# Expert tiles past the 24th moved into one of eight code arms, chosen at run time by the number of tiles in use

## The chip, the cores and the metric

The kernel runs on one core of a Trainium2 chip. A core has five engines with an instruction queue each: TensorE (PE, whose weight loads the profile lists apart as PEld), VectorE (DVE), ScalarE (ACT), GpSimd (POOL) and SyncE (SP), beside 16 DMA engines. Each queue is read in order by a sequencer of its engine, and work on different engines is ordered by semaphores. The metric is the device time of one execution in microseconds; the kernel before takes 641.05 us (median of three runs, 640.5 to 641.71).

## The reference, cut to what matters

Two stages, all in float32. A causal linear attention with a decay per head makes `x` of 4 x 768 tokens with 512 channels. A mixture of experts with 8 experts follows, in which a token either takes the expert with its largest logit or keeps the expert of the token before it:

```python
for s in range(S):
    fresh_e = int(np.argmax(logits[b, s]))
    if s == 0 or local_gate[b, s] < 0.5:
        e = fresh_e
    else:
        e = prev_e if prev_e >= 0 else fresh_e
    prev_e = e
    ...
    h = np.maximum(x[b, s] @ w1[e], 0.0)      # 512 -> 1024
    out[b, s] = p[e] * (h @ w2[e])            # 1024 -> 512
```

Which expert gets how many of the 3072 tokens is known only when the kernel runs. With the reference's inputs its routing gives the eight experts 410, 373, 371, 423, 434, 362, 354 and 345 tokens. In tiles of 128 tokens, of one expert each, that is 4, 3, 3, 4, 4, 3, 3 and 3: 27 tiles. Any routing needs between 24 (`NT`) and 31 (`G`) tiles.

## The kernel before, in words

Three stages follow each other.

**Attention** (lines 103 to 249): 24 steps of 128 tokens. SP loads q, k and v, PE does the matmuls, and each step writes 128 rows of `x` to the buffer `x_dram` in device memory and leaves 9 logits per token.

**Routing** (lines 252 to 385): one chain of small DVE and PE operations. It finds every token's expert, gives each expert whole tiles, and leaves three tables with a column per tile: `gidx` (which row of `x_dram` stands in each place of the tile), `sidx` (where the result goes; an unused place has an index past the end, which the store skips) and `gate`, and a row `owner` with each tile's expert. `ends` holds the running sum of the experts' tiles, so its last column is the number of tiles in use.

**Experts** (lines 388 to 447): a loop over all 31 tiles, unrolled when the program is built. For tile g:

- `gather(g)` (line 402, POOL): an indirect DMA brings 128 rows of `x_dram` into `xg`, one of three buffers.
- `turn` (line 409, PE; line 411, DVE): four transposes into `ptm`, copied to `xtm`.
- `hidden` (line 421, PE; line 423, ACT): 32 matmuls into `ph`, in two halves, each followed by a Relu into `ht`.
- `output` (line 429, PE; line 431, DVE; line 432, POOL): 8 matmuls into `py`, a multiplication with the gate into `y`, and an indirect DMA that stores `y`'s rows in the output.
- `weights(g)` (lines 394 to 398, SP): loads the tile's expert number into a register and issues two DMAs of 2 MB for `w1` and `w2`, into one of two buffers by the parity of g. The condition `other` skips them where that buffer holds this expert already.

The order on each engine comes from a scheduler that sees the whole unrolled loop; on PE it is `ph` of tile g, `ptm` of tile g+1, `py` of tile g. A float32 matmul of the program stands in the profile as two weight loads and two matmuls, a transpose as one of each; so PE's `ph` of one tile is 64 matmul records, `py` 16 and `ptm` 4. Tiles 27 to 30 are computed like the others: their gather reads row 0 for every place, and their store skips every row.

Of the kernel before, what the change touches and what calls it, by code (L numbers as in the profile page):

```python
# [9 lines left out]
I32 = mybir.dt.int32  # L10
U32 = mybir.dt.uint32
ACT = mybir.ActivationFunctionType
ALU = mybir.AluOpType
# [10 lines left out]
E, F = 8, 1024  # L24
DT, FT = DM // P, F // P
N = B * S
NT = N // P
# [4 lines left out]
G = (N + E * (P - 1)) // P  # L32
# [7 lines left out]
def kernel(  # L40
# [9 lines left out]
    nc = tc.nc  # L50
    const = ctx.enter_context(tc.tile_pool(name="const", bufs=1))
    wts = ctx.enter_context(tc.tile_pool(name="wts", bufs=1))
    route = ctx.enter_context(tc.tile_pool(name="route", bufs=1))
# [9 lines left out]
    def w1_src(e):  # L63
        return w1[bass.ds(e, 1)].rearrange("o (t p) f -> p (o t) f", p=P)

    def w2_src(e):
        return w2[bass.ds(e, 1)].rearrange("o (t p) d -> p (o t) d", p=P)
# [46 lines left out]
    with tc.tile_pool(name="build", bufs=1) as build:  # L114
# [10 lines left out]
        for u in range(2):  # L125
            rows = slice(DH * u, DH * u + DH)
# [126 lines left out]
    sidx = route.tile([P, G], U32, name="sidx")  # L253
    gate = route.tile([P, G], F32, name="gate")
    owner = route.tile([1, G], I32, name="owner")
    with tc.tile_pool(name="rt", bufs=1) as rt, tc.tile_pool(name="pr", bufs=1, space=PSUM) as pr:
        lg = lt[:, :, :E]
        mx = rt.tile([P, NT], F32, name="mx")
# [67 lines left out]
        more = rt.tile([P, E, NT], F32, name="more")  # L326
        nc.vector.tensor_tensor(more, incl[:, :, NT - 1:NT].broadcast_to([P, E, NT]),
                                whole.unsqueeze(1).broadcast_to([P, E, NT]), ALU.is_gt)
        tiles = rt.tile([P, E], F32, name="tiles")
        nc.vector.tensor_reduce(tiles, more, axis=AX.X, op=ALU.add)  # L330
        ends = rt.tile([P, E], F32, name="ends")
# [23 lines left out]
        own = rt.tile([1, G, E], F32, name="own")  # L355
# [3 lines left out]
        nc.vector.tensor_reduce(own1, own, axis=AX.X, op=ALU.add)  # L359
        nc.vector.tensor_scalar(own1, own1, float(E - 1), None, ALU.min)  # L360
        nc.vector.tensor_copy(owner, own1)


        val = rt.tile([P, NT, 2, G], F32, name="val")
# [28 lines left out]
    def weights(g):  # L393
        e = experts[g] = nc.values_load(owner[0:1, g:g + 1], engines=[SP], min_val=0, max_val=E - 1,
                                        skip_runtime_bounds_check_because="an index of 8 experts")
        other = e != experts[g - 2]
        nc.sync.dma_start(out=w1t[g % 2], in_=w1_src(e), cond=other, cond_hint=False)
        nc.sync.dma_start(out=w2t[g % 2], in_=w2_src(e), cond=other, cond_hint=False)

    def gather(g):  # L400
        xg = moe.tile([P, DM], F32, name="xg", bufs=3)
        nc.gpsimd.indirect_dma_start(out=xg, out_offset=None, in_=x_dram[:, :],  # L402
                                     in_offset=bass.IndirectOffsetOnAxis(ap=gidx[:, g:g + 1], axis=0))
        return xg

    def turn(xg):
        pt = pm.tile([P, DT, P], F32, name="ptm")
        for d in range(DT):
            nc.tensor.transpose(pt[:, d], xg[:, P * d:P * d + P], ident)  # L409
        xt = moe.tile([P, DT, P], F32, name="xtm")  # L410
        nc.vector.tensor_copy(xt, pt)  # L411
        return xt

    def hidden(g, xt):
        ht = moe.tile([P, FT, P], F32, name="ht")
        for half in range(2):
            ph = pm.tile([P, FT // 2, P], F32, name="ph")
            for i in range(FT // 2):
                f = FT // 2 * half + i
                for d in range(DT):  # L420
                    nc.tensor.matmul(ph[:, i], lhsT=w1t[g % 2][:, d, P * f:P * f + P], rhs=xt[:, d],  # L421
                                     start=(d == 0), stop=(d == DT - 1))
            nc.scalar.activation(ht[:, FT // 2 * half:FT // 2 * half + FT // 2], ph, ACT.Relu)  # L423
        return ht

    def output(g, ht):
        py = pm.tile([P, DM], F32, name="py")
        for f in range(FT):
            nc.tensor.matmul(py, lhsT=ht[:, f], rhs=w2t[g % 2][:, f], start=(f == 0), stop=(f == FT - 1))  # L429
        y = moe.tile([P, DM], F32, name="y")  # L430
        nc.vector.tensor_scalar(y, py, gate[:, g:g + 1], None, ALU.mult)  # L431
        nc.gpsimd.indirect_dma_start(out=out, out_offset=bass.IndirectOffsetOnAxis(ap=sidx[:, g:g + 1], axis=0),  # L432
                                     in_=y, in_offset=None, bounds_check=N - 1, oob_is_err=False)

    weights(0)
    weights(1)
    rows = {g: gather(g) for g in range(2)}
    xt = turn(rows.pop(0))
    for g in range(G):
        if g + 2 < G:  # L440
            rows[g + 2] = gather(g + 2)
        ht = hidden(g, xt)
        if g + 1 < G:
            xt = turn(rows.pop(g + 1))
        output(g, ht)
        if g + 2 < G:
            weights(g + 2)


# [32 lines left out]
```

## Time and profile before

| | |
|---|---|
| median of three runs | 641.05 us (640.5 to 641.71) |
| the profiled execution: its own time | 640.74 us |
| its span, first to last instruction | 639.0 us |
| mean granted TensorE clock | 0.965 |
| instructions | 9717 |
| PE busy | 590.9 us, 92% of the span |
| DVE, ACT, POOL busy | 126.3, 72.6 and 130.4 us |
| attention and routing, to the first `ph` | 0 to 182.7 us |
| 31 expert tiles on PE | 182.7 to 631.0 us |
| after PE's last matmul | 631.0 to 639.0 us |

Busy time of PE is the time in which matmuls are in flight; the granted clock is the share of full speed that the chip allowed. In a row of a timeline stand start and length in us, engine, line, operation, and behind it in brackets how long the engine was idle before and what ended that. An engine's name with a q (SPq, POOLq, PEldq) is its sequencer: waits, register loads and branches, which are not counted as busy.

### The profile page before, as it was taken

Reading aid. Unit: us, or ns where it says so; the run is one execution under the profiler, and the core shown is the slowest. Engines: PE = TensorE matmul, PEld = TensorE weight load, DVE = VectorE, ACT = ScalarE, POOL = GpSimd, SP = SyncE. Lnnn points to the kernel's source line nnn. Section 1 sums busy time; section 2 is a strip of 40 time slices with the busy share of each in tenths; the row PEclk is TensorE's granted clock in tenths of the full one; section 3 lists DMA queues with packets and bytes.
Section 4 is the critical chain, followed back from the end, with each engine's and each line's share of the span. In section 5 each row is a group of like instructions: output and inputs, shape, how many; then the busy total and the mean of one; then the engine's idle time right before and its main releaser. Section 6 shows DMA issues by size and latency. Waiting matters only on the chain. (4 is left out here: it accounts for less than half of the span.)

```text
span 639.0 us, 9717 instructions
## 1 busy us (share of the span) xinstructions
PE 590.9 (92%) x4104; PEld 449.3 (70%) x4104; DVE 126.3 (20%) x269; ACT 72.6 (11%) x136; POOL 130.4 (20%) x149
## 2 busy tenths in 40 slices
PE   4989889894669999999999999999999999999994
PEld 4777777773667777777777777777777777777772
DVE  6533434326700000100001000100001000010000
ACT  1222222230000000001000000000101000000100
POOL 4565565300031111111111111111111111111000
PEclk9999999995579999999999999999999999999998
DMA  8999986310020295494691296159379197010000
GB/s 315 361 344 388 379 300 223 117 67 16 2 82 21 86 329 211 167 313 161 236 336 53 67 338 226 34 172 330 130 255 334 50 337 252 34 34 12 0 1 1
DMA packets 37675, 113.63 MB, mean 178 GB/s; under 512 B 3390, under 2 KB 3390, under 8 KB 34560
## 3 DMA queue, kind: packets, MB, share of 16 engines
q1 hardware_dynamic: 29216, 92.30, 40.6%
q0 software_dynamic: 4960, 14.43, 6.5%
q10 hardware_dynamic: 3456, 6.29, 2.6%
q8 instruction: 32, 0.52, 0.3%
q14 instruction: 11, 0.09, 0.0%
HBM read 171.73 MB, written 14.42 MB: 291 GB/s over the span
## 5 line engine op out<-in xcount | busy, mean ns | idle before, releaser
L421 PEld LDWEIGHTS ph<-xtm,w 128*128 128x128 f32 x1984 | 227.5, 193 | 14.4 <-issue 14.4
L421 PE MATMUL ph<-xtm,w 128*128 128x128 f32 x1984 | 227.7, 276 | 0.0
L429 PE MATMUL py<-w,ht 128*128 128x512 f32 x496 | 218.0, 592 | 0.0
L429 PEld LDWEIGHTS py<-w,ht 128*128 128x128 f32 x496 | 91.8, 190 | 103.8 <-issue 103.8
L423 ACT ACTIVATE ht<-ph 128x512 f32<-128x512 f32 x62 | 37.0, 597 | 442.4 <-PE ph L421 442.4
L432 POOL DMA_INDIRECT out_dram<-y,sidx x31 | 31.4, 1014 | 242.2 <-DVE y L431 242.2
L402 POOL DMA_INDIRECT xg<-x_dram,gidx x31 | 30.3, 978 | 200.9 <-PE ptm L409 140.3
L431 DVE TENSOR_SCALAR y<-py,gate 128x512 f32<-128x512 f32 x31 | 23.3, 751 | 206.8 <-PE py L429 206.8
L411 DVE COPY xtm<-ptm 128x512 f32<-128x512 f32 x31 | 21.5, 693 | 204.6 <-PE ptm L409 204.6
L174 DVE TENSOR_TENSOR sm<-ps,mask 128x512 f32<-128x512 f32 x48 | 30.9, 686 | 34.6 <-PE ps L171 34.5
L171 PE MATMUL ps<-inp 64*128 64x128 f32 x384 | 29.7, 297 | 8.4 <-DMA inp<-in_qkv_dram 8.4
L156 POOL TENSOR_TENSOR qd<-inp,lamq 128x512 f32<-128x512 f32 x20 | 25.5, 1274 | 44.6 <-PE po L184 29.8
L171 PEld LDWEIGHTS ps<-inp 64*128 64x128 f32 x384 | 24.9, 199 | 13.0 <-DMA inp<-in_qkv_dram 8.7
L188 PE MATMUL po<-sm,inp 128*64 128x128 f32 x384 | 27.1, 285 | 0.0
L409 PE MATMUL ptm<-ident,xg 128*128 128x128 f32 x124 | 19.6, 283 | 6.0 <-DMA xg<-x_dram,gidx 6.0
L159 POOL TENSOR_TENSOR kd<-inp,rev 128x512 f32<-128x512 f32 x20 | 20.8, 1043 | 13.2 <-DVE rev L138 6.3
L188 PEld LDWEIGHTS po<-sm,inp 128*64 128x64 f32 x384 | 21.2, 140 | 3.0 <-issue 0.2
L184 PE MATMUL po<-qd,kv 128*128 128x128 f32 x160 | 23.2, 288 | 0.0
L197 PE MATMUL pk<-inp,kd 128*128 128x128 f32 x160 | 23.2, 288 | 0.0
L191 ACT COPY xt<-po 128x512 f32<-128x512 f32 x24 | 14.1, 586 | 75.3 <-PE po L188 75.3
L197 PEld LDWEIGHTS pk<-inp,kd 128*128 128x128 f32 x160 | 19.4, 191 | 3.6 <-issue 3.3
L184 PEld LDWEIGHTS po<-qd,kv 128*128 128x128 f32 x160 | 19.4, 191 | 2.5 <-issue 0.2
(107 smaller groups left out, 204.2 us busy)
## 6 DMA issues: line engine op xcount, KB each, us to landing
w<-in_w_dram SPq DMA_DIRECT2D x66, 2048.0 KB
inp<-in_qkv_dram SPq DMA_DIRECT2D x24, 1024.0 KB
x_dram<-xn ACTq DMA_DIRECT2D x24, 256.0 KB
xg<-x_dram,gidx POOLq DMA_INDIRECT x31, 3.9
out_dram<-y,sidx POOLq DMA_INDIRECT x31, 2.8
wgt<-in_wg_dram SPq DMA_DIRECT2D x1, 18.0 KB
lamb<-in_lam_dram SPq DMA_DIRECT2D x1, 4.0 KB
```

The lines of the kernel that those rows point to most:

```text
L156: nc.gpsimd.tensor_tensor(qd, x[:, 0].rearrange("p (a i) -> p a i", i=P), lamq, ALU.mult)
L171: nc.tensor.matmul(ps[u][:, a], lhsT=kt[rows, a], rhs=qt[rows, a], start=True, stop=True)
L174: nc.vector.tensor_tensor(sm[:, u], ps[u], mask[:, u], ALU.mult)
L184: nc.tensor.matmul(po[:, a], lhsT=kv[:, a].rearrange("p u d -> p (u d)"), rhs=qd[:, a], start=(a == 0), stop=False, skip_group_check=True)
L188: nc.tensor.matmul(po[DH * u:DH * u + DH, a], lhsT=vn[:, a, u], rhs=sm[:, u, a], start=(not c and a == 0), stop=(a == A - 1), skip_group_c ...
L197: nc.tensor.matmul(pk[:, a], lhsT=kd[:, cols], rhs=x[:, 3, cols], start=True, stop=True)
L402: nc.gpsimd.indirect_dma_start(out=xg, out_offset=None, in_=x_dram[:, :], in_offset=bass.IndirectOffsetOnAxis(ap=gidx[:, g:g + 1], axis=0))
L421: nc.tensor.matmul(ph[:, i], lhsT=w1t[g % 2][:, d, P * f:P * f + P], rhs=xt[:, d], start=(d == 0), stop=(d == DT - 1))
L423: nc.scalar.activation(ht[:, FT // 2 * half:FT // 2 * half + FT // 2], ph, ACT.Relu)
L429: nc.tensor.matmul(py, lhsT=ht[:, f], rhs=w2t[g % 2][:, f], start=(f == 0), stop=(f == FT - 1))
L431: nc.vector.tensor_scalar(y, py, gate[:, g:g + 1], None, ALU.mult)
L432: nc.gpsimd.indirect_dma_start(out=out, out_offset=bass.IndirectOffsetOnAxis(ap=sidx[:, g:g + 1], axis=0), in_=y, in_offset=None, bounds_c ...
```

## The change

The loop is cut in two. The first 23 tiles (0 to 22) stay in straight code, which also gathers tiles 23 and 24, transposes tile 23 and loads the weights of tiles 23 and 24. A new one-element tile `extra` holds the number of tiles in use less 24. Every engine loads it into a register (line 448 of the changed kernel) and takes one of eight arms of code: arm k computes tiles 23 to 23 + k and then branches to the program's end. With 27 tiles in use, arm 3 runs with tiles 23 to 26, and tiles 27 to 30 are not computed. The arms hold the same operations as the loop before; inside one, the gather of tile g + 1 is written ahead of the `hidden` of tile g, and is asked for from tile 25 on.

```diff
+    extra = route.tile([1, 1], I32, name="extra")
...
         nc.vector.tensor_copy(owner, own1)
+        nc.vector.tensor_scalar(extra, ends[0:1, E - 1:E], -float(NT), None, ALU.add)
...
-    for g in range(G):
-        if g + 2 < G:
-            rows[g + 2] = gather(g + 2)
+    for g in range(NT - 1):
+        rows[g + 2] = gather(g + 2)
         ht = hidden(g, xt)
-        if g + 1 < G:
-            xt = turn(rows.pop(g + 1))
+        xt = turn(rows.pop(g + 1))
         output(g, ht)
-        if g + 2 < G:
-            weights(g + 2)
+        weights(g + 2)
+    more = nc.values_load(extra[0:1, 0:1], min_val=0, max_val=G - NT,
+                          skip_runtime_bounds_check_because="at most G tiles")
+    for k in tc.Switch(more, G - NT + 1):
+        last = NT + k
+        own, x = dict(rows), xt
+        for g in range(NT - 1, last):
+            if NT + 1 <= g + 1 < last:
+                own[g + 1] = gather(g + 1)
+            ht = hidden(g, x)
+            if g + 1 < last:
+                x = turn(own.pop(g + 1))
+            output(g, ht)
+            if NT < g + 2 < last:
+                weights(g + 2)
```

On DVE one operation, `extra`, is new in the routing, behind the copy to `owner`; up to tile 22 the order on all engines is otherwise the one before. What moves stands at three places.

PE between tiles 22 and 23, before (`w_0_70` is w2 in the even tiles' buffer, `w_1_69` w1 in the odd tiles'; in brackets the semaphores that an instruction waits for):

```order
L409 MATMUL ptm<-ident,xg 128x128 [waits DMASW2_49]
L409 MATMUL ptm<-ident,xg 128x128 x3
L429 MATMUL py<-w_0_70,ht 128x512 [waits DMAHW3_49,Activation_49]
L429 MATMUL py<-w_0_70,ht 128x512 x3
L429 MATMUL py<-w_0_70,ht 128x512 [waits Activation_49]
L429 MATMUL py<-w_0_70,ht 128x512 x3
L421 MATMUL ph<-xtm,w_1_69 128x128 [waits DMAHW4_49,DVE_49]
L421 MATMUL ph<-xtm,w_1_69 128x128 x15
```

The same place in the changed kernel:

```order
L431 MATMUL py<-w_0_70,ht 128x512 [waits Activation_49]
L431 MATMUL py<-w_0_70,ht 128x512 x3
L448 TENSOR_LOAD extra [waits DVE_49]
L492 SWITCH_STRIDE
L492 ISA x2
L450 BRANCH_PREFETCH_HINT
L423 MATMUL ph<-xtm,w_1_69 128x128 [waits DVE_49,DMAHW4_49,PE_49]
L423 MATMUL ph<-xtm,w_1_69 128x128 x15
```

Between the last `py` of tile 22 and the first `ph` of tile 23 now stand the register load, the jump (two register moves, one fused register operation and an indirect branch) and a hint for the branch at the arm's end; all of them are the sequencer's. The other four engines get the same five instructions behind their last work of tile 22: ACT behind its second Relu, DVE behind `y`, POOL behind the store, SP behind the DMA of tile 24's `w2`.

POOL in arm 3, which stands behind the store of tile 22 and the jump (`ISA` is here an instruction that adds to a DMA semaphore, so that every arm leaves the same counts):

```order
L450 BRANCH_PREFETCH_HINT
L492 ISA [waits DMASW0_49]
L404 DMA xg<-x_dram,gidx 128x512 [waits DMASW0_49,PE_49]
L492 ISA [waits DMASW1_49]
L404 DMA xg<-x_dram,gidx 128x512 [waits DMASW2_49,PE_49]
L492 ISA [waits DMASW2_49]
L434 DMA out_dram<-y,sidx 3072x512 [waits DMASW7_49,DVE_49]
```

Before, the gathers of tiles 25 and 26 stood ahead of the stores of tiles 21 and 22; now both stand at the head of the arm, behind the store of tile 22.

POOL at the end of arm 3, ahead of the program's closing barrier:

```order
L434 DMA out_dram<-y,sidx 3072x512 [waits DMASW4_49,DMASW3_49,DVE_49]
L492 ISA [waits DMASW5_49]
L434 DMA out_dram<-y,sidx 3072x512 [waits DMASW4_49,DVE_49]
L450 ISA [waits DMASW7_49,DMASW6_49]
L492 UNCONDITIONAL_BRANCH
```

The last store is tile 26's instead of tile 30's, and behind it come one more addition to semaphores and the branch to the program's end.

## The prediction, made before the changed kernel was run

> **What bounds the kernel now.** I read the page first: its span, PE's share and the DMA line.
>
> ```profile
> span 639.0 us, 9717 instructions
> PE 590.9 (92%) x4104; PEld 449.3 (70%) x4104; DVE 126.3 (20%) x269; ACT 72.6 (11%) x136; POOL 130.4 (20%) x149
> ```
>
> PE is busy for 92% of the span and no other engine for more than 20%, so the stage that the change cuts was read next from PE alone: its timeline from tile 22 on, then a table of stretches of one tile each.
>
> ```profile
> 501.27 7.31 PE L421 MATMUL ph<-xtm,w 128*128 128x128 f32 x64
> 508.42 0.60 PE L409 MATMUL ptm<-ident,xg 128*128 128x128 f32 x4
> 508.85 7.03 PE L429 MATMUL py<-w,ht 128*128 128x512 f32 x16
> 515.72 7.31 PE L421 MATMUL ph<-xtm,w 128*128 128x128 f32 x64
> ...
> 616.87 7.31 PE L421 MATMUL ph<-xtm,w 128*128 128x128 f32 x64
> 624.01 7.03 PE L429 MATMUL py<-w,ht 128*128 128x512 f32 x16
> ```
>
> ```profile
> core 0: us, PE busy (x) PEld busy (x) DVE busy (x) ACT busy (x) POOL busy (x), PEclk, DMA share, GB/s
> 559.07:573.52 14.45, 14.45 (x85) 10.62 (x84) 1.44 (x2) 1.19 (x2) 1.99 (x2) 1.00 0.12 37
> 573.52:587.97 14.45, 14.45 (x85) 10.62 (x84) 1.44 (x2) 1.19 (x2) 1.02 (x1) 1.00 0.03 13
> 587.97:602.42 14.45, 14.45 (x85) 10.62 (x84) 1.44 (x2) 1.19 (x2) 1.00 (x1) 1.00 0.01 1
> 602.42:616.87 14.45, 14.45 (x85) 10.62 (x84) 1.44 (x2) 1.19 (x2) 0.98 (x1) 1.00 0.01 1
> ```
>
> Tile 22 starts at 501.27 and tile 30 at 616.87: (616.87 - 501.27) / 8 = 14.45 us per tile, and in such a stretch PE is busy for all 14.45 us at a granted clock of 1.00. Nothing waits for data; the expert stage costs exactly its number of tiles. The last column shows which tiles are empty: tile 26's store falls in the stretch from 573.52 (13 GB/s x 14.45 us = 0.19 MB, some 90 rows of 2 KB), the next stretches move 1 GB/s. So the trace, too, has 27 tiles with rows.
>
> **The change part by part.**
>
> *Four tiles fewer on PE.* 4 x 14.45 = 57.8 us leave the path that sets the end. PE's own idle time is nil there, so nothing else than PE's work can come off.
>
> *The selector.* One more DVE operation in the routing chain, between these two:
>
> ```profile
> 159.29 0.16 DVE L360 TENSOR_SCALAR own<-own 1x31 f32<-1x31 f32 x1
> 159.39 0.36 DVE L342 TENSOR_TENSOR place<-place,hot 128x192 f32<-128x192 f32 x1
> ```
>
> A small operation takes 0.16 us, and the next starts 0.10 us later where it doesn't depend on it. DVE runs without a pause there and PE waits for it, so this is on the path: +0.10 to +0.16, I take +0.15.
>
> *The jump on PE.* Nothing before jumps into other code, so its price is bounded from rows of the same instructions on SP, and from PE's code loading:
>
> ```profile
> L394 SPq TENSOR_LOAD <-owner x31: 263/269/473, 159.9 to 588.3; - x31
> L397 SPq FUSED_REGOPS  x31: 50/50/65, 160.6 to 588.7; - x31
> L397 SPq MOVE w<-in_w_dram x31: 29/29/38, 160.7 to 588.9; - x31
> q8 instruction: 32, 0.52, 0.3%
> DMA to landing us min/median/max: 3.3/3.9/7.3
> ```
>
> The register load is 0.27 us (0.47 at most), two moves and a fused operation about 0.11: 0.4 us, at most 0.6. Then code. PE has 4104 + 4104 instructions and 32 code packets of 0.52 MB / 32 = 16 KB, so a packet holds 256 instructions, and arm 3 stands behind three arms: it must be fetched. A packet is under way for 0.3% x 16 x 639 / 32 = 0.96 us; a whole transfer from issue to landing takes 3.9 us (7.3 at most) for the gathers of `xg`, the last row. From both ends the jump takes 0.4 + 0.96 = 1.4 to 0.6 + 7.3 = 7.9 us. I take 0.4 + 3.9 = 4.3, since a fetch has an issue and a landing like any DMA.
>
> How much of it PE feels depends on how far PE's sequencer runs ahead:
>
> ```profile
> L421 PEldq EVENT_SEMAPHORE  x31: 51/51/51, 181.8 to 610.4; - x31
> L478 PEldq DRAIN  x2: 13/3112/6212, 624.9 to 638.6; - x2
> ```
>
> The wait ahead of tile 30's `ph`, which stands right behind tile 29's `py` like the jump behind tile 22's, is passed at 610.4, and that `ph` starts at 616.87: 6.4 us ahead. The drain behind the very last `py` is reached at 624.9 and ends 6.2 us later with PE's work (624.01 + 7.03 = 631.04). So the sequencer has 6.0 to 6.4 us of queued matmuls under which to jump. With 4.3 us the cost on PE is 0, with 7.9 us it is 1.5 to 1.9, and if the cover is gone it is the whole 1.4 to 7.9. I take 0; a gain is excluded, since PE has no idle time to lose.
>
> [...]
>
> *The jump on the other engines.* Their next work after it, in the timeline of the same place before:
>
> ```profile
> 515.92 0.75 DVE L431 TENSOR_SCALAR y<-py,gate 128x512 f32<-128x512 f32 x1 [6.18 <-PE py L429]
> 523.50 0.69 DVE L411 COPY xtm<-ptm 128x512 f32<-128x512 f32 x1 [6.83 <-PE ptm L409]
> ...
> 516.95 1.02 POOL L432 DMA_INDIRECT out_dram<-y,sidx  x1 [6.69 <-DVE y L431]
> ...
> 515.91 0.38 SPq L398 DMA_DIRECT2D w<-in_w_dram  x1
> 523.06 0.37 SPq L397 DMA_DIRECT2D w<-in_w_dram  x1
> 530.37 0.37 SPq L398 DMA_DIRECT2D w<-in_w_dram  x1
> ...
> 537.32 0.60 PE L409 MATMUL ptm<-ident,xg 128*128 128x128 f32 x4
> ```
>
> DVE reaches its jump at 515.92 and is due at 523.50; 515.92 + 4.3 = 520.2. At 7.9 it is 0.3 us late for a copy that PE needs at 530.17, one tile on. SP comes from the DMA at 515.91 and is due at 523.06: at 7.9 it is 0.8 us late with a load of tile 25's weights, for which PE comes at 544.62; 523.06 and 530.37 are the last two real loads (0.37 us to issue; a skipped one takes 0.08), so the arm still has this one to do. ACT's last Relu of tile 22 is at 508.62, its next at 519.55. POOL is latest: its store at 516.95 takes 1.0, the jump ends at 522.3 (525.9 at most), and only then go the gathers of tiles 25 and 26. PE transposes tile 25 at 537.32; 522.3 + 3.9 = 526.2 (525.9 + 7.3 = 533.2 at most). All are hidden by PE's work on tiles 23 and 24, some 29 us, and cost 0. If that cover were gone, the gather would put its 1.0 + 4.3 + 3.9 us on the path.
>
> *The end.* After PE's last matmul come `y`, the store and POOL's drain:
>
> ```profile
> 632.11 0.98 POOL L432 DMA_INDIRECT out_dram<-y,sidx  x1 [13.03 <-DVE y L431]
> L478 POOLq DRAIN  x3: 40/107/6353, 631.9 to 638.8; - x3
> DMA to landing us min/median/max: 2.1/2.8/8.5
> ```
>
> Before, the last store moves no row and lands after the least time, 2.1 us; tile 26's moves 89 rows, so I take the median, 2.8: +0.7. The addition to semaphores and the branch behind it stand ahead of the drain, which has 6.35 us of its own running; they cost 0, and at most another 6.35 if the drain has to begin behind them.
>
> *Sum.* 639.0 - 57.8 + 0.15 + 0 + 0.7 = 582.05 us of span. Around the span lie 640.74 - 639.0 = 1.74, so 583.8 for a profiled execution; the median of the three runs is 0.31 above the profiled one: **584.1 us**. With no landing cost and 0.10 for the selector it is 583.3; with 1.9 us of jump seen, 586.0.
>
> **The rivals.**
>
> *PE stands still at the jump.* If a register load or a jump must wait until PE's queue is empty, nothing covers it: 584.1 + 4.3 = 588.4, and 585.5 to 592.0 by the bounds. For it: no row before has PE load a register or jump. Against it: the 6.2 and 6.4 us above, at instructions in that very position. Chance 0.15.
>
> *The pause also halves PE's clock.*
>
> ```profile
> 144.00:185.02 41.02, 21.91 (x95) 0.50 0.11 33
> ...
> 182.69 8.42 PE L421 MATMUL ph<-xtm,w 128*128 128x128 f32 x64
> ```
>
> In the routing, with PE working half the time, the clock was 0.50; it came back at 185.02, some 2.3 us into tile 0's `ph`, which took 8.42 instead of 7.31 us. So a fall costs some 1.1 us on top of a pause: 588.4 + 1.1 = 589.5. Against it: it needs the first rival, and the rows do not show how short a pause is enough. [...] Chance 0.08.
>
> *The end grows.* If POOL's drain starts only behind the addition and the branch, or the arm's exit has to fetch code (3.9), the 6.35 us come later: 584.1 + 3.9 = 588.0, up to 590.5. For it: POOL ends last already. Against: landing and drain run beside what is added. Chance 0.07.
>
> *The change does not cut.* If the number in the register were that of the last arm, all 31 tiles would run behind a jump: 641.05 + 0.15 + 0 to 7.9 = 641.2 to 649.1. Against it: 27 tiles by the rows of the stores. Chance 0.03, a third of it within 0.2%.
>
> *Slower: the arm's code arrives block by block.* Arm 3 has 4 x 40 matmuls of four instructions and 3 x 4 transposes of two, 664 in all or 2.6 blocks of 256. If in an arm each of 3 blocks were fetched only when PE stands still for it, the change would lose from 57.0 / 3 = 19 us a block on. Against it: a packet takes 0.96 us, and 7.3 us a block would still give 584.1 + 21.9 = 606.0. In straight code PE uses up a block in 14.45 x 256 / 168 = 22 us without a pause. Chance 0.01.
>
> **How the numbers follow.** The forecast, jump hidden and end nearly unchanged, has 0.66: the row of the sequencer's lead speaks for it directly, the fetch time is the part that no row shows. Its own range is 583.0 to 586.0 (the sum's ends, less 0.3 for the spread of a median). Two in ten may be left out: the range goes from 583.0 to 590.2, which takes in both pauses at 4.3 us and nearly all of the growing end. A measurement of this kernel tells differences over about 0.2% (1.3 us) from none. Faster: all cases but the last two, 0.96; within 0.2%: 0.01, from the selector; slower: 0.02 + 0.01 = 0.03.
>
> **What would show it.** Right: PE's matmuls fall from 4104 to 4104 - 4 x 84 = 3768 records (64 of `ph`, 16 of `py` and 4 of `ptm` a tile); `ph` of tile 23 starts 515.72 - 508.85 = 6.87 us after tile 22's `py`, as before; PE's register load of `extra` starts some 6.4 us before that `ph`; four tiles follow at 14.45 us; the last `py` ends at 631.04 - 57.8 + 0.15 = 573.4; from there to the end it is 8.0 to 8.7 us. Wrong: an idle time of PE ahead of tile 23's `ph` released by "issue" or by PE's sequencer (the jump is seen, and its length is the price), a `ph` of 8.4 us there (the clock fell), a wait of `ptm` for `xg` at tile 25 (POOL came late), a stretch over 8.7 us behind the last `py` (the end grew), or 4104 matmuls (nothing was cut). The forecast fails if the register load stands near the end of `py` instead of near its beginning: then the lead that hides the jump isn't there.

## The result, and the profile after

The changed kernel takes **585.06 us** (median of four runs, 584.13 to 586.49) against 640.77 us (640.21 to 641.71) of the kernel before: a ratio of 0.913, interval 0.9106 to 0.9156. The prediction was 584.1 us with a range of 583.0 to 590.2. It holds, but the profile shows that three parts of it were off by 1 to 3 us each and nearly cancel in the execution profiled.

The first lines of the page:

```profile
span 582.4 us, 8992 instructions
...
PE 531.2 (91%) x3768; PEld 404.7 (69%) x3768; DVE 120.5 (21%) x262; ACT 67.8 (12%) x128; POOL 122.2 (21%) x141
```

PE has 3768 matmul records, which is 4104 - 4 x 84: four tiles are gone, as asked for. Where the time went is read from a table of stretches, cut at the same events in both kernels: the start of tile 0's `ph`, of tile 22's, of tile 23's, the end of the last `py`, and the end. In a row stand the stretch, its length, then the busy time of each engine, the granted clock, the DMA share and GB/s. Before:

```profile
0.00:182.69 182.69, 142.55 (x1508) 119.87 (x1509) 82.22 (x208) 35.58 (x74) 72.64 (x91) 0.89 0.61 224
182.69:501.27 318.58, 318.58 (x1845) 234.41 (x1845) 31.01 (x43) 26.27 (x44) 42.80 (x43) 1.00 0.55 193
501.27:515.72 14.45, 14.45 (x85) 10.62 (x84) 1.44 (x2) 1.19 (x2) 1.99 (x2) 1.00 0.45 165
515.72:631.05 115.33, 115.33 (x669) 84.36 (x667) 10.86 (x15) 9.55 (x16) 11.96 (x12) 1.00 0.23 77
631.05:639.04 7.99, 0.00 (x0) 0.00 (x0) 0.75 (x1) 0.00 (x0) 0.98 (x1) 0.78 0.01 1
```

After:

```profile
0.00:180.13 180.13, 140.41 (x1509) 117.86 (x1509) 82.24 (x209) 35.54 (x74) 72.20 (x91) 0.91 0.61 227
180.13:498.73 318.60, 318.60 (x1846) 234.42 (x1845) 30.97 (x43) 26.27 (x44) 42.02 (x43) 1.00 0.55 192
498.73:514.33 15.60, 14.62 (x86) 10.47 (x84) 2.19 (x3) 1.19 (x2) 1.01 (x1) 1.00 0.44 154
514.33:571.93 57.60, 57.60 (x332) 41.94 (x332) 4.33 (x6) 4.78 (x8) 5.95 (x6) 1.00 0.41 138
571.93:582.42 10.49, 0.00 (x0) 0.00 (x0) 0.75 (x1) 0.00 (x0) 0.98 (x1) 0.64 0.06 21
```

Row by row: attention and routing are 2.56 us shorter, although the change adds an operation there; 22 tiles take the same; the stretch with the jump is 1.15 us longer (15.60 - 14.45); from tile 23 on 115.33 - 57.60 = 57.73 us are saved, and PE is busy for all of the 57.60; the end is 2.50 us longer (10.49 - 7.99). -2.56 + 0.02 + 1.15 - 57.73 + 2.50 = -56.62, which is the difference of the spans, 582.42 - 639.04.

**The jump on PE.** PE's timeline around it:

```profile
506.31 7.03 PE L431 MATMUL py<-w,ht 128*128 128x512 f32 x16
514.33 7.38 PE L423 MATMUL ph<-xtm,w 128*128 128x128 f32 x64 [0.98 <-DVE y L433]
```

Tile 23's `ph` starts 514.33 - 506.31 = 8.02 us after `py`, not 6.87, and PE idles for 0.98 us. The releaser named, DVE's `y`, did not hold PE up, it is the other event nearby: with the early hint below, the same `ph` starts at 513.24 us, before its `y` at 513.45. The sequencers' own rows tell why, in three groups: the register load (line 448), the jump (line 492) and the hint that is the first instruction of the arm (line 450). They give count, shortest, median and longest in ns, and when the first and the last start:

```profile
L448 PEldq TENSOR_LOAD <-extra x1: 485/485/485, 506.7 to 506.7; - x1
```

```profile
L492 PEldq COMPARE_BRANCH  x2: 327/3333/6339, 507.6 to 565.8; - x2
L492 DVEq COMPARE_BRANCH  x2: 60/64/69, 514.2 to 572.0; - x2
```

```profile
L450 PEldq BRANCH_PREFETCH_HINT  x1: 50/50/50, 514.0 to 514.0; - x1
L450 DVEq BRANCH_PREFETCH_HINT  x1: 56/56/56, 520.5 to 520.5; - x1
```

Each engine branches twice, into the arm and out of it. PE's branch into the arm starts at 507.6 and takes 6.34 us, and the arm's first instruction follows at 514.0. On the other engines the stall does not stand in the branch's row but between the branch and the hint: DVE 514.2 to 520.5, ACT 506.8 to 512.6, SP 514.3 to 520.7, POOL 515.0 to 520.7. From the register load to the arm PE's sequencer needs 514.0 - 506.7 = 7.3 us, with 513.34 - 506.74 = 6.6 us of queued matmuls ahead of it. 7.3 + 0.33 to the first matmul - 6.6 = 1.0, the idle time.

**The end.** The timeline of its last rows, then POOL's sequencer:

```profile
571.96 0.75 DVE L433 TENSOR_SCALAR y<-py,gate 128x512 f32<-128x512 f32 x1 [13.26 <-PE py L431]
572.99 0.98 POOL L434 DMA_INDIRECT out_dram<-y,sidx  x1 [13.03 <-DVE y L433]
```

```profile
L450 POOLq INC_SWDGE_SEM  x1: 1262/1262/1262, 572.8 to 572.8; - x1
```

```profile
L492 POOLq DRAIN  x3: 40/113/4566, 577.0 to 582.1; - x3
...
L492 POOLq COMPARE_BRANCH  x2: 38/54/70, 515.0 to 574.1; - x2
```

The store ends at 573.97, the addition to the DMA semaphores (`INC_SWDGE_SEM`) holds POOL's sequencer until 574.1, the branch out of the arm starts there, and the drain only at 577.0, 2.9 us later. It then takes 4.57 us. Between branch and drain, at 575.4, two code packets of 8 KB start, whose record doesn't name the engine. Before, the drain was running from 631.9 on, beside the store.

**The clock in the early stages.** Most of the 2.56 us comes from where the granted clock changes: the attention ends 1.31 us earlier (the first `prow` starts at 144.98 instead of 146.29), of which 0.2 were there before the first step of the clock, and `pe` of the routing takes 1.70 instead of 2.72 us. Stretches between the clock's steps, for PE alone, of the changed kernel:

```profile
core 0: us, PE busy (x), PEclk, DMA share, GB/s
8.00:11.77 3.77, 3.33 (x30) 1.00 1.02 428
11.77:144.89 133.12, 118.28 (x1398) 1.00 0.74 276
144.89:148.30 3.41, 2.72 (x12) 0.50 0.00 0
148.30:151.72 3.42, 1.16 (x11) 1.00 0.00 0
151.72:182.44 30.72, 16.98 (x75) 0.50 0.13 35
```

and of the kernel before:

```profile
14.36:144.06 129.70, 117.01 (x1378) 1.00 0.74 274
144.06:185.02 40.96, 21.91 (x95) 0.50 0.11 32
```

The 1.00 of the row from 8.00 is no measurement; the records of the clock begin with the step at its end. 133.12, 30.72 and 40.96 us are 39, 9 and 12 times 3.413 us, so the steps lie on a grid. Here the first step to full speed came at 11.77 us, in the kernel before at 14.36, and one grid step of the routing ran at full clock. Which place the grid has against the kernel's start differs from execution to execution: in the last experiment the same kernel has its first step at 15.64 us.

### The profile page after: what moved, and what is told of

Read it like the earlier page. It is cut to its first block, busy times and chain, and to the rows that moved or that the text cites. A ratio compares the mean times of both kernels' runs of the same rounds, so it can differ in the third digit from the quotient of the medians.

```text
span 582.4 us, 8992 instructions
## 1 busy us (share of the span) xinstructions
PE 531.2 (91%) x3768; PEld 404.7 (69%) x3768; DVE 120.5 (21%) x262; ACT 67.8 (12%) x128; POOL 122.2 (21%) x141
## 4 chain that ended last, share of the span: by engine, by line
PE 63%; issue 7%; DMA 3%; DVE 3%; another core or an unknown queue 1%; ACT 0%; POOLq 0%; POOL 0%
PE ph L423 28%; PE py L431 27%; DMA out_dram<-y,sidx 2%; PE ptm L411 2%; PE pinv L377 2%; PE po L184 1%; PE po L188 1%; DMA xg<-x_dram,gidx 1%; PE ps L171 1%; PE prow L279 0%; PE pt L212 0%; PE pl L227 0%; DVE run L287 0%; PE pe L291 0%
## 5 line engine op out<-in xcount | busy, mean ns | idle before, releaser
L423 PEld LDWEIGHTS ph<-xtm,w 128*128 128x128 f32 x1728 | 198.2, 193 | 13.8 <-issue 13.7
L423 PE MATMUL ph<-xtm,w 128*128 128x128 f32 x1728 | 198.5, 276 | 1.0 <-DVE y L433 1.0
L431 PE MATMUL py<-w,ht 128*128 128x512 f32 x432 | 189.9, 592 | 0.0
L431 PEld LDWEIGHTS py<-w,ht 128*128 128x128 f32 x432 | 80.0, 190 | 90.4 <-issue 90.4
L425 ACT ACTIVATE ht<-ph 128x512 f32<-128x512 f32 x54 | 32.2, 597 | 389.4 <-PE ph L423 389.4
L434 POOL DMA_INDIRECT out_dram<-y,sidx x27 | 27.3, 1010 | 220.8 <-DVE y L433 220.8
L404 POOL DMA_INDIRECT xg<-x_dram,gidx x27 | 26.4, 977 | 172.5 <-PE ptm L411 123.9
L433 DVE TENSOR_SCALAR y<-py,gate 128x512 f32<-128x512 f32 x27 | 20.3, 751 | 182.1 <-PE py L431 182.1
L413 DVE COPY xtm<-ptm 128x512 f32<-128x512 f32 x27 | 18.7, 691 | 178.2 <-PE ptm L411 178.2
L411 PE MATMUL ptm<-ident,xg 128*128 128x128 f32 x108 | 17.2, 284 | 5.7 <-DMA xg<-x_dram,gidx 5.7
```

## The experiments

Times are compared with the kernel before on the same chip. One stage is free of what the grid does to the early stages: from tile 22's start to the end. This table of the profiled executions has it, with the two parts that are in question (times in us, read from the timelines; where the arms begin at tile 22, tile 21 to 22 stands in the third column):

| kernel | tile 0 starts | tile 22 to 23 | last `py` to end | tile 22 to end |
|---|---|---|---|---|
| before | 182.69 | 14.45 | 7.99 | 137.77 |
| changed | 180.13 | 15.60 | 10.49 | 83.69 |
| straight code for 27 tiles | 183.35 | 14.45 | 7.34 | 79.31 |
| changed, beside straight code | 181.10 | 15.81 | 10.51 | 83.93 |
| no weights for tile 24 | 180.50 | 14.45 | 10.51 | 82.48 |
| early hint | 180.58 | 14.45 | 10.44 | 82.42 |
| last store behind the arms | 183.41 | 15.37 | 7.40 | 80.37 |
| hint and last store | 183.70 | 14.45 | 7.38 | 79.36 |
| all 31 tiles through the jump | 181.45 | 15.43 | 8.05 | 138.88 |
| arms from tile 22 | 181.09 | 14.45 | 8.86 | 80.84 |
| used arm last | 181.86 | 16.37 | 8.06 | 82.04 |
| used arm first | 179.97 | 14.45 | 10.46 | 82.43 |
| changed, beside the two orders of arms | 183.16 | 15.70 | 10.44 | 83.74 |

### What the arms cost: straight code for 27 tiles, and the changed kernel beside it

```diff
-    for g in range(G):
-        if g + 2 < G:
+    for g in range(27):
+        if g + 2 < 27:
             rows[g + 2] = gather(g + 2)
```

This is the kernel before with 27 in place of `G` in the loop: no selector, no jump, no arms.

> Edit: no jump and no selector; the loop is written for 27 tiles and the program is straight code (it only holds for this routing). It measures what the jump and the arms cost beside the cut. If the profile of the changed kernel is to be believed (first ph of tile 23 1.15 us later than a tile's pitch, the stretch after the last matmul 10.5 instead of 8.0 us, selector 0.15), this kernel is 3.1 to 3.8 us faster than the changed one: a span of some 639.0 - 57.8 = 581.2 with before's early stages, 8.0 to 8.7 us after the last matmul. Rival: the jump costs next to nothing in the median and the 2.5 us by which the changed kernel's experts began earlier belong to the change: then the two differ by less than 1 us, or this one is slower.

The changed kernel ran beside it:

> The changed kernel as it is, once more, beside its variants on the same chip. Expected: 584 to 586.5 us; PE's branch record at the jump about 6.3 us, PE idle about 1 us ahead of tile 23's ph, 10.5 us from the last matmul to the end. If the jump depends on what else the DMA engines move, its length varies from run to run by tenths of a microsecond; if it is a fixed price, it is the same to 0.1 us.

Measured: straight code 582.21 us (579.56 to 583.34), ratio 0.909 (0.9064 to 0.912); the changed kernel 585.84 us, ratio 0.917 (0.9146 to 0.9197). Of the 585.84 - 582.21 = 3.6 us the table shows 1.15 to 1.36 at the jump and 3.15 at the end (10.49 - 7.34); from tile 22 on it is 83.69 - 79.31 = 4.38 us. The medians hold the early stages too, so the two differences need not be the same. The end of straight code:

```profile
575.36 0.98 POOL L432 DMA_INDIRECT out_dram<-y,sidx  x1 [13.03 <-DVE y L431]
```

```profile
L479 POOLq DRAIN  x3: 40/107/5698, 575.1 to 581.4; - x3
```

The drain starts beside the store and ends at 580.8, 4.5 us behind the store's end. A last store with real rows makes the end no longer: it is 0.65 us shorter than before (7.34 to 7.99). So the arms alone, not the rows, cost the changed kernel its end.

### Why the jump takes 6.3 us: other transfers, place, or the branch itself

At the jump the weights of tile 24 are being loaded. The first experiment leaves out these two transfers, so that tiles 24 and 26 are computed with another expert's weights:

```diff
     def weights(g):
+        if g == NT:
+            return
```

> Edit: the two weight DMAs of tile 24, which run while the jump waits for its code, are left out (so tiles 24 and 26 are computed with another expert's weights; the amount of work is the same). Theory 1, the code packets queue behind weight packets: the branch records of PE and ACT fall from 6.3 and 5.8 us to about 2.8 us (what the branches out of the arm took with idle DMA engines), those of DVE, SP and POOL as well; PE's idle time ahead of tile 23's ph goes to 0 and the time falls by 1.0 to 1.2 us. Rival, the jump's 6.3 us are its own: branch records and time as in the changed kernel.

Measured: 584.44 us (582.63 to 586.44), ratio 0.914 (0.9115 to 0.9166). PE's branch, and the DMA engines during it (columns as above), without these transfers:

```profile
L494 PEldq COMPARE_BRANCH  x2: 341/2018/3696, 507.9 to 564.8; - x2
```

```profile
507.89:511.59 3.70, 3.70 (x10) 1.00 0.04 9
```

and in the changed kernel:

```profile
507.60:513.94 6.34, 5.74 (x14) 1.00 0.87 322
```

With the DMA engines 4% busy the branch takes 3.7 us (more than the 2.8 that was expected), with 87% it takes 6.3. The records of the single packets show where the 2.6 us go: PE's code packet of 16 KB starts 3.9 us after the branch where weights are under way, 1.0 us where they are not, and is itself under way for 1.1 and 1.3 us. So beside the weights it is the start of the fetch that comes later, by 2.9 us. At 3.7 us the branch fits below the queued matmuls (6.6 us), and PE's idle time is gone (14.45).

The same with all the work in place: the arms begin one tile earlier, where the next weights are skipped because the buffer has them.

```diff
-    for g in range(NT - 1):
+    for g in range(NT - 2):
...
-        for g in range(NT - 1, last):
-            if NT + 1 <= g + 1 < last:
+        for g in range(NT - 2, last):
+            if NT <= g + 1 < last:
...
-            if NT < g + 2 < last:
+            if NT <= g + 2 < last:
```

> The changed kernel with the loop cut one tile earlier: tiles 0 to 21 straight, the arms from tile 22. At that place no weights of 2 MB are under way for most of the jump (tile 23 takes tile 21's expert, its load is skipped), so if the fetch is slow because its packets stand behind the weights' in the DMA engines, PE's branch takes 3.5 to 4.5 us instead of 6.3 to 6.5, PE's idle time ahead of tile 22 is under 0.3 us, and the kernel is 1.0 to 1.4 us below the changed one, with the end as long as before (10.5 us). Rival (the price is that of the jump's own work or of the arm's distance, whatever the DMA engines do): branch 6 us or more, PE idle 0.8 to 1.3 us ahead of tile 22, and the same time as the changed kernel within 0.5 us.

Measured: 583.07 us (581.34 to 584.98), ratio 0.911 (0.9086 to 0.9134); PE's branch 3.68 us, no idle time of PE, 14.45 us from tile 21 to 22.

```profile
493.50:497.18 3.68, 3.68 (x10) 1.00 0.04 9
```

The price is that of the place. One expectation failed: the end was to stay at 10.5 us and is 8.86. In this program no addition to the semaphores stands behind the last store, so that POOL's branch is taken at 571.9, ahead of the store (572.16 to 573.14), and the 2.6 us from there to the drain at 574.5 lie partly beside the store.

The third way asks for the arm's code early. The selector is loaded into the registers in the routing, and every engine gets a hint for the jump there:

```diff
+    more = nc.values_load(extra[0:1, 0:1], min_val=0, max_val=G - NT,
+                          skip_runtime_bounds_check_because="at most G tiles")
     for g in range(NT - 1):
+        if g == NT - 2:
+            tc.switch_hint({e: more for e in [PE, SP, mybir.EngineType.DVE, mybir.EngineType.Activation, mybir.EngineType.Pool]}, G - NT + 1, "arms")
...
-    for k in tc.Switch(more, G - NT + 1):
+    for k in tc.Switch(more, G - NT + 1, hint="arms"):
```

> Edit: every engine loads the selector already in the routing and is given a prefetch hint for the arm, some 320 us ahead of the jump. Theory 2, the jump waits for code and a hint fetches it: the branch records at the jump fall below 1 us, PE's idle time ahead of tile 23's ph goes to 0, the time falls by 1.0 to 1.2 us less some 0.5 us for register loads in the routing. Rival: a hint given many code blocks ahead is lost again, then the branch records stay at 6 us on PE; on ACT, DVE, SP and POOL, whose whole expert stage is one or two blocks, it may work all the same.

Measured: 584.83 us (582.93 to 585.39), ratio 0.914 (0.9114 to 0.9165). Though the hint is written at tile 22, the scheduler put it where the selector was ready:

```profile
L446 PEldq BRANCH_PREFETCH_HINT  x1: 48/48/48, 156.9 to 156.9; - x1
```

```profile
L494 PEldq COMPARE_BRANCH  x2: 298/322/346, 507.1 to 564.6; - x2
```

PE's branch takes 0.35 us instead of 6.3, 350 us after the hint, and PE has no idle time. That does not mean that the code came 350 us early. PE's code packets of the whole execution (packets, MB, share), in the changed kernel and with the hint:

```profile
q8 instruction: 32, 0.52, 0.3%
```

```profile
q8 instruction: 31, 0.51, 0.3%
```

Ahead of the jump both have 27, at the same places of the program: the first one behind the hint starts at 166.5 us (167.5 in the changed kernel), 9.6 us after it, and the last at 498.5 (499.9). Behind the jump the changed kernel has one more, that of 511.5 us, within the branch (507.6 to 513.9). So the hint added no packet. Whether one of the 27 carries the arm's code, and which one, no record says. The author's estimate is the last, 8.6 us ahead of the jump: between tile 0 and the jump the packets of the changed kernel stand 21.9 us apart on average (14 steps from 193.6 to 499.9), so that the jump would leave the block at hand before the one fetched last is due, and the hint would change what the last fetch brings. No run shows it.

The last one changes only the order of the arms: that of 27 tiles is now the first, right behind the jump.

```diff
-        nc.vector.tensor_scalar(extra, ends[0:1, E - 1:E], -float(NT), None, ALU.add)
+        nc.vector.tensor_scalar(extra, ends[0:1, E - 1:E], -3.0 - float(NT), None, ALU.add)
...
-        last = NT + k
+        last = NT + (k + 3) % 8
```

> The changed kernel with the arm for 27 tiles as the first of the eight, right behind the jump, and the selector shifted to match. If the code behind the jump is fetched ahead like straight code, PE's branch to it takes 0.3 to 1 us, PE is not idle ahead of tile 23, and the time is 1.0 to 1.4 us below the changed kernel's, with the end at 10.5 us. Rival (an indirect branch always throws the fetched code away, as near as its target may be): branch 6.2 to 6.5 us on PE, 5.8 to 6.4 on the others, PE idle 0.9 to 1.4 us, and the same time as the changed kernel within 0.5 us.

Measured: 584.83 us (582.66 to 586.89), ratio 0.914 (0.9115 to 0.9158), beside 586.17 us of the changed kernel on that chip.

```profile
L492 PEldq COMPARE_BRANCH  x2: 317/322/327, 507.4 to 564.3; - x2
```

Both branches of PE now take 0.3 us, and PE does not idle. So an indirect branch is not dear as such: into the arm right behind it PE's takes 0.33 us at most, into the one behind three other arms 6.34. That the near arm's code was there already is the author's reading, which no row here shows.

### Why the end takes 10.5 us

Two explanations stood against each other: the exit branch fetches the end's code ahead of the drain, or the drain waits for the landing of the last rows. The first experiment moves the last store behind the arms, so that POOL leaves the arm while PE still works:

```diff
-        y = moe.tile([P, DM], F32, name="y")
+        y = end if end is not None else moe.tile([P, DM], F32, name="y")
...
+        if end is not None:
+            return
...
-            output(g, ht)
+            if g == last - 1:
+                nc.vector.tensor_copy(slast, sidx[:, g:g + 1])
+            output(g, ht, ylast if g == last - 1 else None)
...
+    nc.gpsimd.indirect_dma_start(out=out, out_offset=bass.IndirectOffsetOnAxis(ap=slast[:, 0:1], axis=0),
+                                 in_=ylast, in_offset=None, bounds_check=N - 1, oob_is_err=False)
```

> The changed kernel with one thing moved: the last tile's y is written to a tile of its own, DVE copies that tile's column of sidx to one place, and the one store of the last tile stands behind the join of the arms, in the block of the program's end, so POOL's exit branch comes ahead of the store and not behind it. Theory (the end's extra 2.5 to 3.2 us are the fetch of the end block, which stands between store and drain): POOL branches while PE still works on the last tile, the fetch is hidden, the store follows y at once and the drain the store; from the last matmul to the end it is 7.3 to 8.0 us as in straight code instead of 10.5, the drain ends 4.5 to 5.1 us behind the store, and the time is 2.5 to 3.1 us below the changed kernel's of the same chip. Rival (the drain's length follows the landing of the last store with real rows, wherever the code lies): the end stays at 10 to 10.5 us and the time within 0.5 us. The jump to the arm stays as it is: branch on PE 6.3 to 6.5 us, PE idle 1.0 to 1.3 us.

Measured: 582.75 us (580.74 to 584.19), ratio 0.909 (0.9068 to 0.9116), and from the last `py` to the end 7.40 us.

```profile
576.14 0.98 POOL L468 DMA_INDIRECT out_dram<-ylast,slast  x1 [13.03 <-DVE ylast L433]
```

```profile
L500 POOLq DRAIN  x3: 40/118/5708, 575.9 to 582.2; - x3
...
L500 POOLq COMPARE_BRANCH  x2: 38/54/70, 518.3 to 563.2; - x2
```

The exit branch is at 563.2, some 12 us before PE is done, and the drain runs beside the store again. The same rows land in the same way; so not their landing made the end long, but what stood between the store and the drain. That is the addition to the semaphores (1.26 us), which is now ahead of the store too, and what fills the 2.9 us from branch to drain, by the author's reading the fetch. PE's branch was 6.1 us here and its idle time 0.76, a little under what was expected.

Then all 31 tiles through the jump, with the selector held at 7:

```diff
-        nc.vector.tensor_scalar(extra, ends[0:1, E - 1:E], -float(NT), None, ALU.add)
+        nc.vector.tensor_scalar(extra, ends[0:1, E - 1:E], 0.0, float(G - NT), ALU.mult, ALU.add)
```

> The changed kernel with the selector set to 7, so that all 31 tiles are computed through the jump, like before: what is left is the price of the arms without the cut. Theory, from the rows of the changed kernel: 0.15 us for the selector, 1.0 to 1.4 us of PE idle at the jump, 2.5 to 3.2 us at the end: 3.7 to 4.8 us over the kernel before, ratio 1.006 to 1.0075; the arm of 8 tiles stands first or last among the arms, and its distance makes no difference. Rival (the nearness of prediction and result is real, the jump and the end are nearly hidden): within 0.8 us of the kernel before, ratio 0.999 to 1.001.

Measured: 641.38 us (638.8 to 643.14), ratio 1.001 (0.999 to 1.0025): the theory's 3.7 to 4.8 us are not there. The jump cost what was expected (15.43 instead of 14.45 us); the end did not.

```profile
L492 POOLq DRAIN  x3: 40/118/5895, 631.7 to 638.1; - x3
...
L492 POOLq COMPARE_BRANCH  x2: 38/54/70, 515.8 to 631.2; - x2
```

From the exit branch at 631.2 to the drain at 631.7 it is 0.5 us instead of 2.9, and the end is 8.05 us. Three things differ here: this arm is the last in the code and the end's block follows it, its last store carries no rows, and no addition stands behind that store. The next experiment changes the first alone, by making the arm of 27 tiles the last:

```diff
-        nc.vector.tensor_scalar(extra, ends[0:1, E - 1:E], -float(NT), None, ALU.add)
+        nc.vector.tensor_scalar(extra, ends[0:1, E - 1:E], 4.0 - float(NT), None, ALU.add)
...
-        last = NT + k
+        last = NT + (k + 4) % 8
```

> The changed kernel with the arms in another order: the arm for 27 tiles is the last of the eight in the code, right ahead of the end block, and the selector is shifted to match; the work is the same, and the addition to the DMA semaphores behind the last store stays. Theory (the end is long because the exit branch of an inner arm has to fetch the end block; with the selector at 7 the drain followed the exit branch after 0.4 us and the end was 8.05 us): here the exit needs no fetch, POOL's drain starts 0.2 to 0.6 us behind the branch instead of 2.9, the end is 7.4 to 8.2 us instead of 10.5, and the time 2.3 to 3.1 us below the changed kernel's. Rival (the end was short there because the last tile had no rows, or because that arm has no addition behind its last store): the end is 8.9 us or more; with the addition as the sole cause it stays 10.5 us. The jump stays: PE's branch 6.2 to 6.5 us, PE idle 0.9 to 1.4 us.

Measured: 583.76 us (583.44 to 584.04), ratio 0.911 (0.9092 to 0.9128), 2.4 us below the changed kernel on that chip; the end is 8.06 us.

```profile
L492 POOLq DRAIN  x3: 40/113/4552, 576.9 to 582.0; - x3
...
L492 POOLq COMPARE_BRANCH  x2: 38/54/70, 516.4 to 576.4; - x2
```

With the same rows and the same addition the drain follows the branch after 0.5 us. So of the 3.15 us that the end has over straight code, 10.49 - 8.06 = 2.4 go with the arm's place in the code, and are put down to the fetch, and 8.06 - 7.34 = 0.7 are the addition and the branch, which stand between store and drain here as well. What was not foreseen: PE's branch took 7.12 us and PE idled for 1.76. With weights under way the price of the jump varies, 6.1 to 7.1 us over the six profiled kernels that jump at this place without a hint into an arm that is not the first.

### Both mended

The early hint and the moved store together:

> The moved store and the early hint together: selector loaded in the routing, the arm's code asked for there, last store behind the join. If the two costs are separate and there is no third one, this kernel equals straight code for 27 tiles (582.2 us where the kernel before took 638.7) plus 0.15 us for the selector: ratio to the kernel before 0.909 to 0.911, the end 7.3 to 8.0 us, tile 22 to tile 23 14.45 us on PE. If the costs overlap (the hint's code already pays for the end's), it gains no more than the moved store alone. If something else in the arm costs time, such as the additions to the semaphores, it stays 1 us or more above straight code, and the pitch of tiles 23 to 26 or the start of tile 23 shows it.

Measured: 582.70 us (579.83 to 584.17), ratio 0.909 (0.9059 to 0.9115). Jump 14.45, end 7.38, and from tile 22 to the end 79.36 us, against 79.31 of straight code and 83.69 of the changed kernel. From tile 22 on the jump and the end are all that the arms cost; nothing third is left. On this stage the version is 4.3 us faster than the changed kernel, and it still has an arm for every number of tiles. The two were not timed on one chip; their intervals of the ratio (0.9059 to 0.9115, and 0.9106 to 0.9156) overlap a little, so that the times alone do not separate them.

### The early stages

> The changed kernel as it is, as the measure for the two others on this chip: PE's branch 6.2 to 6.5 us, PE idle 0.9 to 1.4 us ahead of tile 23, the end 10.5 us. The start of tile 0 and with it the whole time may lie 2 to 3 us to either side, by where the steps of the granted clock fall in the attention and the routing; theory: their grid of 3.4 us keeps its spacing and only its place against the start of the kernel differs. Rival: the steps fall at the same place in each execution of one kernel, and the start of tile 0 then differs from the 180.1 and 181.1 us seen so far by under 0.2 us from one of them.

Measured: 586.17 us (583.9 to 587.58), ratio 0.914 (0.9112 to 0.916). The same kernel as in the first profile, and tile 0 starts at 183.16 instead of 180.13 us:

```profile
8.00:15.64 7.64, 7.17 (x55) 1.00 1.02 428
15.64:145.35 129.71, 116.09 (x1371) 1.00 0.73 271
145.35:186.31 40.96, 22.72 (x99) 0.50 0.11 32
```

The first step to full clock is at 15.64 instead of 11.77, and in the routing the half clock stays for twelve grid steps (40.96 us) without the break at 148. 129.71 us are 38 steps of 3.413. Over all profiled kernels a first step at 11.5 to 12.1 us goes with a start of tile 0 at 180.0 to 181.5, one at 13.1 to 14.4 with 181.9 to 182.7, and one at 15.3 to 15.8 with 183.2 to 183.7, whatever the kernel. In both executions of the changed kernel the stretches between steps are whole multiples of 3.413 us (39, 1, 1 and 9; 38 and 12), while the first step lies 15.64 - 11.77 = 3.87 us apart: the spacing of the grid is the same, its place against the start of the kernel is not. Thus single executions differ by some 3 us before any expert tile runs (183.16 - 180.13 = 3.03), and differences of about 1 us between two kernels, like the one at the jump, are read from the stages' rows and not from the medians.

## Why the prediction was right or wrong

- **Four tiles fewer, -57.8 us: right.** From tile 23 on 57.73 us are saved, PE is busy without a gap, and the clock stays at 1.00. Neither the arm's code, block by block, nor a late gather of tile 25 held it up.
- **The jump: mechanism right, size off.** That the sequencer runs ahead and hides the jump was right: its lead was 6.6 us where 6.0 to 6.4 were read off. The failed term is the 4.3 us, 0.4 for registers and one median landing of 3.9; measured are 7.3, of which the branch is 6.3, inside the bounds of 1.4 to 7.9. The prediction's own rule, length less lead, then gives about the 1.0 us that PE idled. The 3.9 us came from gathers over all stages; the jump falls just where 2 MB of weights keep the DMA engines 87% busy. With them 4% busy the branch takes 3.7 us, and the forecast of a hidden jump holds.
- **PE stands still at the jump, and the clock falls: both refuted.** The register load ran at 506.74, 0.43 us into `py`, and the stretch has a clock of 1.00.
- **The other engines' jumps: right.** They took 2.8 us more than priced (DVE 513.4 to 520.5, 7.1 instead of 4.3); no engine made PE wait from tile 23 on.
- **The end: wrong term and a rival underrated.** The +0.7 for a last store with rows had the wrong sign: straight code shows -0.65. The addition and the branch, put at 0 because landing and drain would run beside them, stand ahead of the drain: 0.7 us, and 2.4 more for the exit's fetch. Together 2.5 over before. This is the rival "the end grows", given 0.07, with a price of 3.15 us over straight code instead of 3.9. The argument against it failed because POOL's drain still took 4.54 to 4.57 us in each kernel where it started behind the store, so a late start shows almost in full.
- **The selector, +0.15: too much.** `extra` takes 0.13 us, but the scheduler put it further ahead than the program has it, at 156.33, ahead of the copy to `owner` and between two operations of the chain. From the start of `own<-ends,count` to that of the first `val` it is 158.86 - 155.93 = 2.93 us, against 161.17 - 158.26 = 2.91 before: 0.02 us.
- **The sum.** Jump and end add 1.15 + (2.50 - 0.7) = 2.95 us to the forecast; the early stages took 2.56 + 0.15 = 2.7 off it in this execution. That the profiled 584.13 lies so close to the 583.8 worked out for it is chance. In the two later measurements the changed kernel had 585.84 and 586.17 us.

## What to carry to other kernels

The jump into an arm further off cost PE 6.1 to 7.1 us here beside weight loads and 3.7 with the DMA engines 4% busy: price a jump in the traffic of its place, give a hint for it ahead (here one in the routing was enough, 0.35 us; how near to the jump it may stand was not tried) or put the likely arm right behind the jump (0.33 us), and compare its length with the queued work of the engine that sets the end. Look as hard at the way out as at the way in: the exit branch between the last store and the closing drain had no work above it here, and 2.4 of the 2.9 us from branch to drain showed. Where a clock grid moves the early stages by microseconds (here tile 0 starts at 179.97 to 183.70 us), cut the profiles at common events before believing that a sum came out.

## What the runs showed of the hardware that was not expected

- The branch to an arm behind others takes 6.1 to 7.1 us on PE beside weight loads, 3.7 with the DMA engines 4% busy, and 0.35 with the early hint; to the arm right behind the jump it takes 0.33 at most.
- A hint given 350 us ahead made the branch short without a code packet more: 27 ahead of the jump, with it and without. The hints at the heads of the arms, for the way out, did not do the same for POOL: from its exit branch to the drain it stayed 2.6 to 3.0 us in each kernel whose branch leaves an arm that is not the last and whose store stands in the arm. Why is open.
- A closing drain of POOL that starts beside the last store ends 4.5 us after the end of a store with 89 rows, and 5.1 us after that of a store with none (before: 633.09 to 638.23; all 31 tiles: 632.41 to 637.56). The reason was not looked for. One that starts 0.6 us behind a store with 89 rows (the used arm last) ends 5.2 us after it.
- An addition to the DMA semaphores on POOL takes 0.7 us inside the arm, the one at the arm's end, behind the last store, 1.26.
